# A 4 MB zero fill sent from inside the loop over the heads instead of behind it

## Chip, cores, metric

One core of one Trainium2 chip. The metric is device time in microseconds (us) of one execution. Times are medians, and a comparison is always with runs of the kernel before on the same chip in the same rounds.

## The reference

One decode step of a transformer block and its gradients. Attention has 16 query heads on 8 key/value heads, a cache of 32768 positions of which only the last 4096 are read, and a gated MLP follows. Of the nine outputs two are large: the gradients of the K and V caches, 8 x 32768 x 256 bf16 each. Outside the last 4096 positions they are zero, and these zeros must be written.

```python
W = min(4096, max(256, Sk // 4))                    # 4096 of Sk = 32768
k = jnp.repeat(k_cache[:, :, Sk - W:, :], rep, axis=1)
v = jnp.repeat(v_cache[:, :, Sk - W:, :], rep, axis=1)
scores = jnp.einsum("bhqd,bhkd->bhqk", q, k) * (Dh ** -0.5)
p = _softmax(scores, axis=-1)
o = jnp.einsum("bhqk,bhkd->bhqd", p, v)
...
_out, _vjp = jax.vjp(_f, A_x, A_k_cache, A_v_cache, A_wq, A_wo, B_w_gate, B_w_up, B_w_down)
_grads = _vjp(grad_out)                             # out_2, out_3: the caches' gradients
```

## The kernel before

Most zero fills are sent by GpSimd from a zero buffer of 128 x 8192. The last 18.9 MB of zeros (five transfers, "late fills") are kept back for SyncE, which also sends nearly all loads and all other stores. Four of them read a zero buffer of twice the width; its second half holds data of a V cache until a late memset ("the clearing") makes it zero.

```python
zeros = ar(0, ZW)                                   # ZW = 8192 columns; the second half is ar(ZW, ZW)
late_jobs = [(out_2, G - 1, 5, 7, 2 * ZW), (out_3, G - 1, 0, 6, 2 * ZW), (out_3, G - 1, 6, 7, ZW)]
...                                                 # cut: first pass, MLP, gradients of the small tensors
plan = [[], [], [job_o(0)], [job_o(1)], [job_d, job_q], [expand_dg, job_qB, job_g(0)], [job_g(1)], []]
order = [2, 3, 4, 5, 6, 7, 0, 1]
for it, g in enumerate(order):                      # second pass, one key/value head each
    ...                                             # cut: stV, stK computed by TensorE, VectorE, ScalarE
    for o_ap, st_ in ((out_3, stV), (out_2, stK)):
        LD.dma_start(out=o_ap[0, g, Sk - W:, :].rearrange("(p t) d -> p t d", t=T), in_=st_)
    for job in plan[it]:
        job()                                       # gradients of the weights, made and stored in between
    if it == 6:
        nc.vector.memset(ar(ZW, ZW), 0.0)           # the clearing
...                                                 # cut: GpSimd's last fills
for o, g, n0, n1, f in late_jobs:
    reg = zero_rows(o, g, n0, n1, f)
    for i in range(reg.shape[0]):
        LD.dma_start(out=reg[i], in_=ar(2 * ZW - f, f))
```

`LD` is SyncE's queue; its ring is the line in which its transfers wait for the DMA engines. The two stores of a head are called its pair, and pairs are counted in the order of the loop. The builder is the part of the framework that orders each engine's instructions when the program is built. The drain is the end of the kernel, when nothing computes and the last transfers run.

Of the kernel before, what the change touches and what calls it, by code (L numbers as in the profile page):

```python
# [26 lines left out]
ZW = 8192  # L27
# [7 lines left out]
def kernel(  # L35
# [3 lines left out]
    LD = nc.sync  # L39
# [15 lines left out]
    def ar(off, n):  # L55
        return arena[:, off:off + n]

    def kv_at(off):
        return ar(off, T * Dh).rearrange("p (t d) -> p t d", d=Dh)
# [57 lines left out]
    def zero_rows(o, g, n0, n1, f):  # L117
        reg = o[0, g, 0:Sk - W, :].rearrange("s d -> (s d)")[n0 * 128 * ZW:n1 * 128 * ZW]
        return reg.rearrange("(n p f) -> n p f", p=128, f=f)

    late_jobs = [(out_2, G - 1, 5, 7, 2 * ZW), (out_3, G - 1, 0, 6, 2 * ZW), (out_3, G - 1, 6, 7, ZW)]
    fills = []
    for g in range(G):
        for o in (out_2, out_3):
# [125 lines left out]
    def fill_vpad(i, src):  # L250

        nc.vector.tensor_copy(out=vpad[i][:].rearrange("p e (c w) -> p e c w", w=18)[:, :, :, 0:2],
                              in_=src.unsqueeze(2).to_broadcast([128, 2, 8, 2]))

    def dots(X_sb, XT_slots, pad, rows, cols_pool, cols_tag, evac):

        rows_ps = ps_s.tile([16, 512], f32, tag="rows")
        for q in range(8):
            XT = XT_slots[q % 3]
            tr_ps = ps_tr.tile([128, 2, 4, 128], bf16, tag="tr")  # L260
            for dh in range(2):
                for i in range(4):
                    nc.tensor.transpose(tr_ps[:, dh, i, :], X_sb[:, 4 * q + i, dh * 128:(dh + 1) * 128], ident_bf[:])  # L263
            evac(q, XT, tr_ps[:])
            for dh in range(2):
                nc.tensor.matmul(rows_ps[:], lhsT=pad[:, dh, 16 * q:16 * q + 16], rhs=XT[:, dh].rearrange("p t k -> p (t k)"),  # L266
                                 start=(q == 0 and dh == 0), stop=(q == 7 and dh == 1))
        nc.vector.tensor_copy(out=rows, in_=rows_ps[:])  # L268
        cols_ps = cols_pool.tile([128, 4, 8, 2], f32, tag=cols_tag, name="cols_ps")
        for i in range(4):  # L270
            nc.tensor.transpose(cols_ps[:, i].rearrange("p c h -> p (c h)"), rows[:, i * 128:(i + 1) * 128], ident_f[0:16, 0:16])
        return cols_ps
# [232 lines left out]
    with tc.tile_pool(name="work2", bufs=2) as work2, tc.tile_pool(name="lnw", bufs=1) as lnw, \  # L505
# [109 lines left out]
        for it, g in enumerate(order):  # L615
            V_sb = kv_at(V2_off[it])
            fill_vpad(it % 2, doT_bf[:, :, 2 * g:2 * g + 2])

            def evac(q, XT, ps):
                if q % 2:  # L620
                    nc.scalar.copy(out=XT, in_=ps)  # L621
                else:
                    nc.vector.tensor_copy(out=XT, in_=ps)  # L623
            dpT_ps = dots(V_sb, VT_slot, vpad[it % 2], rows2, ps_t, "tmp", evac)

            pds = work2.tile([128, 4, 8, 4], bf16, tag="pds")
            pv = pT_all[:, g].rearrange("p (q l) h -> p q l h", q=4)
            tmp = work2.tile([128, T, 2], f32, tag="tmp2")
            nc.vector.tensor_tensor(out=tmp[:], in0=dpT_ps[:].rearrange("p q l h -> p (q l) h"),
                                    in1=delta_bc[:, 2 * g:2 * g + 2].unsqueeze(1).to_broadcast([128, T, 2]), op=ALU.subtract)  # L630
            nc.vector.tensor_copy(out=pds[:, :, :, 0:2], in_=pv)
            nc.vector.tensor_tensor(out=pds[:, :, :, 2:4], in0=tmp[:].rearrange("p (q l) h -> p q l h", q=4), in1=pv, op=ALU.mult)
            r_ps = ps_t.tile([128, 128], bf16, tag="tmp")
            nc.tensor.transpose(r_ps[:], pds[:].rearrange("p q l i -> p (q l i)"), ident_bf[:])
            rTm = rT_slot[it % 2]
            nc.vector.tensor_tensor(out=rTm, in0=r_ps[:].unsqueeze(1).to_broadcast([128, 8, 128]),
                                    in1=tl_f[:].unsqueeze(2).to_broadcast([128, 8, 128]), op=ALU.mult)
            nc.vector.tensor_copy(out=Zr, in_=Z4[:, :, :, g, :].rearrange("p w e i -> p (w e) i").unsqueeze(2).to_broadcast([128, 4, 32, 4]))
            R_ps = ps_t.tile([128, 2, 2, 128], f32, tag="tmp")
            for w in range(2):  # L640
                for dh in range(2):
                    nc.tensor.matmul(R_ps[:, w, dh, :], lhsT=Zr[:, 2 * w + dh].rearrange("p k i -> p (k i)"), rhs=ident_bf[:], start=True, stop=True)
            R_sb = R_slot[it % 2]
            nc.scalar.copy(out=R_sb, in_=R_ps[:].rearrange("p w e n -> p (w e n)"))
            stV, stK = V_sb, kv_at(dK_off[it % 2])
            for l in range(8):
                for qp in range(2):
                    d_ps = ps_d.tile([128, 2, 2, Dh], f32, tag="d")
                    for qi in range(2):
                        q = 2 * qp + qi  # L650
                        nc.tensor.matmul(d_ps[:, qi].rearrange("p w d -> p (w d)"), lhsT=rTm[32 * q:32 * (q + 1), l, :], rhs=R_sb[32 * q:32 * (q + 1), :],  # L651
                                         start=True, stop=True)
                    t = 4 * l + 2 * qp
                    if qp:
                        nc.scalar.copy(out=stV[:, t:t + 2, :], in_=d_ps[:, :, 0, :])  # L655
                        nc.scalar.copy(out=stK[:, t:t + 2, :], in_=d_ps[:, :, 1, :])  # L656
                    else:
                        nc.vector.tensor_copy(out=stV[:, t:t + 2, :], in_=d_ps[:, :, 0, :])  # L658
                        nc.vector.tensor_copy(out=stK[:, t:t + 2, :], in_=d_ps[:, :, 1, :])  # L659
# [3 lines that stand above are left out]
                job()  # L663
            if it == 6:

                nc.vector.memset(ar(ZW, ZW), 0.0)

        o, g, i = fills[-1]
        flat = zero_rows(o, g, i, i + 1, ZW)[0].rearrange("p f -> (p f)")
        base = 0  # L670
        for p0, k, m, w in ((0, 5, 2, 288), (20, 3, 8, ZW), (64, 8, 9, ZW - 40), (0, 4, 8, ZW)):
            n = k * m * w
            ZQ.dma_start(out=flat[base:base + n].rearrange("(k m f) -> k m f", k=k, m=m),
                         in_=zeros[p0:p0 + 4 * k - 3:4, 0:w].unsqueeze(1).to_broadcast([k, m, w]))
            base += n
        assert base == 128 * ZW
        for o, g, n0, n1, f in late_jobs:
            reg = zero_rows(o, g, n0, n1, f)
            for i in range(reg.shape[0]):
                LD.dma_start(out=reg[i], in_=ar(2 * ZW - f, f))  # L680

# [1 line left out]
_INS = ['A_x', 'A_k_cache', 'A_v_cache', 'A_wq', 'A_wo', 'B_x', 'B_w_gate', 'B_w_up', 'B_w_down', 'grad_out']  # L683
# [26 lines left out]
```

## Time and profile before

| | before |
|---|---|
| median of 3 runs | 793.49 us (793.12 to 794.23) |
| bytes moved by DMA | 334.75 MB at 423 GB/s |
| DMA engines busy, by stretches of 20 us or more | 0.98 to 1.03 from 20 to 780 us |
| TensorE / VectorE busy | 60% / 52% of the span |
| first late fill sent | 674.95 us |
| the other four sent | 743.93 us |

Read it from the bytes: nothing computes after about 743.5 us, the DMA engines nearly always have work, and the time is nearly bytes over rate. The lines are in the prediction.

### The profile page before, as it was taken

How to read it: one execution, taken by the hardware profiler on the slowest of the kernel's cores; microseconds unless marked ns; L12 is line 12 of the kernel's file. 1: busy time of each engine (PE TensorE's matmuls, PEld its weight loads, DVE VectorE, ACT ScalarE, POOL GpSimd, SP SyncE). 2: the span in 40 equal slices, each digit the busy share in tenths (PEclk: the TensorE clock that was granted, in tenths of full speed). 3: DMA queues.
4: the chain of work that ended last, by engine and by line, in shares of the span. 5: the costliest groups of instructions: out<-in, count | busy, mean ns of one | idle time of the engine just before them, and what ended most of it. 6: DMA issues, size and time to landing. Idle time of an engine off the chain costs nothing.

```text
span 791.1 us, 7239 instructions
## 1 busy us (share of the span) xinstructions
PE 475.9 (60%) x2926; PEld 220.8 (28%) x2926; DVE 410.6 (52%) x621; ACT 196.1 (25%) x309; POOL 29.8 (4%) x41
## 2 busy tenths in 40 slices
PE   0359998999999999453226848583551535363100
PEld 0224333344343433142114714231210211131000
DVE  2105764847658476052884288486680583555300
ACT  0043123141241301000101207372331344134300
POOL 6000000000000000110300000000000000001000
PEclk9987999999999999655556959886556556556555
DMA  9999999999999999999999999999999999999998
GB/s 345 429 432 430 429 430 431 432 431 432 428 427 430 427 427 426 418 420 422 433 431 425 425 425 432 427 429 430 427 426 429 428 427 429 423 428 407 413 439 350
DMA packets 28759, 334.75 MB, mean 423 GB/s; under 512 B 1966, under 2 KB 5046, under 8 KB 6966
## 3 DMA queue, kind: packets, MB, share of 16 engines
q0 software_dynamic: 15904, 216.01, 64.2%
q1 hardware_dynamic: 11382, 116.68, 35.1%
q10 hardware_dynamic: 1440, 1.61, 0.6%
q8 instruction: 23, 0.38, 0.2%
q14 instruction: 10, 0.08, 0.0%
HBM read 53.69 MB, written 280.59 MB: 423 GB/s over the span
## 4 chain that ended last, share of the span: by engine, by line
another core or an unknown queue 40%; DMA 25%; DVE 14%; PE 10%; issue 2%; POOL 2%; ACT 1%; DVEq 0%; ACTq 0%; SPq 0%; POOLq 0%
DMA out_dram<-arena 25%; DVE arena L469 2%; PE rows_ps L266 2%; DVE arena L658 2%; DVE arena L554 2%; PE dqb_ps L512 2%; DVE arena L659 2%; PE d_ps L651 2%; PE tr_ps L263 1%; DVE arena L524 1%; DVE arena L438 1%; POOL out_dram L138 1%; PE dqb_ps L515 1%; DVE arena L623 1%
## 5 line engine op out<-in xcount | busy, mean ns | idle before, releaser
L322 DVE TENSOR_TENSOR arena<-arena,p_f 128x2048 bf16<-128x2048 bf16 x64 | 145.4, 2287 | 64.3 <-PE M_ps L327 64.2
L327 PE MATMUL M_ps<-arena 128*128 128x512 bf16 x512 | 129.3, 381 | 0.2 <-ACT arena L333 0.2
L651 PE MATMUL d_ps<-arena 32*128 32x512 bf16 x256 | 45.4, 521 | 100.6 <-DVE arena L659 85.7
L263 PE MATMUL tr_ps<-ident_bf,arena 128*128 128x128 bf16 x1024 | 92.2, 241 | 20.2 <-DMA arena<-in_A_k_cache_dram 12.7
L266 PE MATMUL rows_ps<-arena,vpad 128*16 128x512 bf16 x256 | 89.5, 445 | 21.4 <-DVE arena L623 15.9
L263 PEld LDWEIGHTS <-arena 128*128 128x128 bf16 x1024 | 68.3, 107 | 74.2 <-issue 60.3
L280 ACT COPY arena<-tr_ps 128x1024 bf16<-128x1024 bf16 x64 | 61.8, 1015 | 70.5 <-PE tr_ps L263 70.5
L330 PE MATMUL ok_ps<-arena 128*16 128x512 bf16 x256 | 64.0, 381 | 0.9 <-DVE arena L307 0.9
L655 ACT CAST arena<-d_ps 128x512 bf16<-128x512 f32 x64 | 37.7, 589 | 106.1 <-PE d_ps L651 106.1
L327 PEld LDWEIGHTS <-arena 128*128 128x128 bf16 x512 | 43.3, 99 | 59.2 <-issue 23.4
L621 ACT COPY arena<-tr_ps 128x1024 bf16<-128x1024 bf16 x32 | 32.5, 1016 | 109.9 <-PE tr_ps L263 35.8
L658 DVE CAST arena<-d_ps 128x512 bf16<-128x512 f32 x64 | 43.9, 686 | 18.2 <-PE d_ps L651 17.7
L659 DVE CAST arena<-d_ps 128x512 bf16<-128x512 f32 x64 | 43.6, 681 | 15.5 <-DMA out_dram<-arena 15.5
L651 PEld LDWEIGHTS <-arena 32*128 32x128 bf16 x256 | 10.7, 96 | 126.0 <-issue 81.9
L656 ACT CAST arena<-d_ps 128x512 bf16<-128x512 f32 x64 | 38.1, 595 | 16.8 <-DMA out_dram<-arena 16.8
L266 PEld LDWEIGHTS <-vpad 128*16 128x16 bf16 x256 | 18.7, 91 | 58.4 <-issue 50.6
L330 PEld LDWEIGHTS <-arena 128*16 128x16 bf16 x256 | 19.1, 89 | 41.6 <-issue 20.5
L549 DVE TENSOR_SCALAR arena<-arena,xT 128x1792 bf16<-128x1792 bf16 (+1 forms) x9 | 7.7, 881 | 37.1 <-DMA out_dram<-arena 37.1
L295 ACT ACTIVATE e_f<-cols_ps,nbias 128x32 f32<-128x32 f32 x16 | 4.5, 286 | 86.9 <-DVE nbias L291 86.9
L524 DVE CUSTOM_DVE_ANT_0 arena<-arena 128x4096 bf16<-128x4096 bf16 x3 | 13.1, 4421 | 23.7 <-ACT arena L517 23.7
L268 DVE COPY arena<-rows_ps 16x512 f32<-16x512 f32 x16 | 10.8, 676 | 27.7 <-PE rows_ps L266 27.7
L623 DVE COPY arena<-tr_ps 128x1024 bf16<-128x1024 bf16 x32 | 21.8, 683 | 3.0 <-PE tr_ps L263 2.5
(198 smaller groups left out, 382.2 us busy)
## 6 DMA issues: line engine op xcount, KB each, us to landing
out_dram<-arena POOLq DMA_DIRECT2D x11, 14336.0 KB, 196.1
out_dram<-arena SPq DMA_DIRECT2D x18, 2048.0 KB, 25.6
out_dram<-arena POOLq DMA_DIRECT2D x15, 2048.0 KB, 54.2
arena<-in_A_v_cache_dram SPq DMA_DIRECT2D x10, 2048.0 KB, 52.8
arena<-in_A_k_cache_dram SPq DMA_DIRECT2D x8, 2048.0 KB, 31.3
out_dram<-arena SPq DMA_DIRECT2D x4, 4096.0 KB, 26.1
out_dram<-arena POOLq DMA_DIRECT2D x1, 12288.0 KB, 43.0
out_dram<-arena POOLq DMA_DIRECT2D x1, 8192.0 KB, 337.3
```

Source lines behind the costliest of these rows:

```text
L263: nc.tensor.transpose(tr_ps[:, dh, i, :], X_sb[:, 4 * q + i, dh * 128:(dh + 1) * 128], ident_bf[:])
L266: nc.tensor.matmul(rows_ps[:], lhsT=pad[:, dh, 16 * q:16 * q + 16], rhs=XT[:, dh].rearrange("p t k -> p (t k)"), start=(q == 0 and dh == 0 ...
L280: sT_ps = dots(kv_at(K_off[g]), KT_slot, vpad[g % 2], rows1, ps_c, "cols", lambda q, XT, ps: nc.scalar.copy(out=XT, in_=ps))
L322: nc.vector.tensor_tensor(out=pK, in0=K_sb[:, 4 * c:4 * c + 4, :].unsqueeze(2).to_broadcast([128, 4, 2, Dh]), in1=p_f[:, c::8, :].unsqueez ...
L327: nc.tensor.matmul(M_ps[:, vh, :], lhsT=V_sb[:, t, vh * 128:(vh + 1) * 128], rhs=pK[:, i, :, :].rearrange("p h d -> p (h d)"), start=(t == ...
L330: nc.tensor.matmul(ok_ps[:].rearrange("p k d -> p (k d)"), lhsT=ppad[g % 2][:, 8 * (t % 4) + t // 4, :], rhs=both(g, t), start=(g == 0 and ...
L621: nc.scalar.copy(out=XT, in_=ps)
L651: nc.tensor.matmul(d_ps[:, qi].rearrange("p w d -> p (w d)"), lhsT=rTm[32 * q:32 * (q + 1), l, :], rhs=R_sb[32 * q:32 * (q + 1), :], start ...
L655: nc.scalar.copy(out=stV[:, t:t + 2, :], in_=d_ps[:, :, 0, :])
L656: nc.scalar.copy(out=stK[:, t:t + 2, :], in_=d_ps[:, :, 1, :])
L658: nc.vector.tensor_copy(out=stV[:, t:t + 2, :], in_=d_ps[:, :, 0, :])
L659: nc.vector.tensor_copy(out=stK[:, t:t + 2, :], in_=d_ps[:, :, 1, :])
```

## The change

The intent is to move one of five late fills out of the tail, into the seventh of eight heads, so that the DMA engines have bytes while the last heads are computed.

```diff
+    late = []
+    for o, g, n0, n1, f in late_jobs:
+        reg = zero_rows(o, g, n0, n1, f)
+        late += [reg[i] for i in range(reg.shape[0])]
...
                 nc.vector.memset(ar(ZW, ZW), 0.0)
+                LD.dma_start(out=late[0], in_=ar(0, 2 * ZW))
...
-        for o, g, n0, n1, f in late_jobs:
-            reg = zero_rows(o, g, n0, n1, f)
-            for i in range(reg.shape[0]):
-                LD.dma_start(out=reg[i], in_=ar(2 * ZW - f, f))
+        for reg in late[1:]:
+            LD.dma_start(out=reg, in_=ar(2 * ZW - reg.shape[1], reg.shape[1]))
```

## The prediction

> **What bounds the kernel now.** I read four views, from coarse to fine. First the page: slices in time, DMA queues and bytes.
>
> ```profile
> DMA  9999999999999999999999999999999999999998
> DMA packets 28759, 334.75 MB, mean 423 GB/s; under 512 B 1966, under 2 KB 5046, under 8 KB 6966
> q0 software_dynamic: 15904, 216.01, 64.2%
> q1 hardware_dynamic: 11382, 116.68, 35.1%
> HBM read 53.69 MB, written 280.59 MB: 423 GB/s over the span
> ```
>
> The row of nines says that the 16 DMA engines are busy in each of the 40 slices, while the page gives TensorE 60% and VectorE 52% of the span. The two queues together take 99.3% of what the DMA engines have; q0 is the one GpSimd fills (the zero fills of the caches' unused part), q1 the one SyncE fills. So the kernel is a stream of 334.75 MB, and time is bytes over rate. To see whether there are holes near the place of the change I cut the last 150 us into stretches.
>
> ```profile
> core 0: us, PE busy (x) PEld busy (x) DVE busy (x) ACT busy (x) POOL busy (x), PEclk, DMA share, GB/s
> 20.00:200.00 180.00, 154.22 (x995) 67.94 (x995) 90.74 (x103) 51.09 (x74) 2.05 (x3) 0.96 1.01 430
> ...
> 660.00:680.00 20.00, 6.44 (x41) 2.72 (x39) 8.93 (x13) 6.59 (x8) 0.00 (x0) 0.67 1.00 426
> 680.00:700.00 20.00, 8.43 (x44) 3.65 (x43) 7.60 (x15) 2.06 (x3) 0.00 (x0) 0.59 1.03 435
> 700.00:720.00 20.00, 15.22 (x103) 7.03 (x102) 14.52 (x25) 11.43 (x19) 2.40 (x4) 0.67 0.98 414
> 720.00:740.00 20.00, 4.56 (x30) 0.90 (x28) 8.87 (x14) 7.62 (x14) 0.00 (x0) 0.50 1.02 415
> 740.00:760.00 20.00, 0.76 (x8) 0.11 (x4) 2.58 (x4) 2.15 (x4) 0.00 (x0) 0.50 1.00 425
> 760.00:780.00 20.00, 0.00 (x0) 0.00 (x0) 0.00 (x0) 0.00 (x0) 0.00 (x0) 0.50 0.99 426
> 780.00:791.10 11.10, 0.00 (x0) 0.00 (x0) 0.00 (x0) 0.00 (x0) 0.00 (x0) 0.50 0.68 289
> ```
>
> The last two columns are what to read: the DMA share stays at 0.98 to 1.03 until 780 us, and only the last 11.1 us have slack (0.68). From about 743 us no engine computes; the kernel drains its last stores and fills.
>
> **Where the fill stands before the change.** The source puts all late fills behind the loop over the heads. The trace shows something else. SyncE's issues in time (start, duration, line):
>
> ```profile
> 652.28 0.33 SPq L609 DMA_DIRECT2D out_dram<-arena  x1
> 674.95 0.33 SPq L680 DMA_DIRECT2D out_dram<-arena  x1
> 675.54 2.32 SPq L661 DMA_DIRECT2D out_dram<-arena  x2
> ...
> 720.87 1.64 SPq L661 DMA_DIRECT2D out_dram<-arena  x2
> ...
> 742.93 0.95 SPq L661 DMA_DIRECT2D out_dram<-arena  x2
> 743.93 5.08 SPq L680 DMA_DIRECT2D out_dram<-arena  x4
> ```
>
> Line 680 is the late fill, line 661 the pair of K and V stores of one head. There are five late fills: four go out at 743.93, behind the last pair, but the first goes out at 674.95, ahead of the pair at 675.54; three pairs of the eight follow it, so that is the sixth head's. The source's order is not the order in which SyncE sends; the framework orders instructions when the program is built, and a fill whose data are ready is free to go. The waits say what held it:
>
> ```profile
> SPq L680 <- DVE arena L666: 22.3, 1, 22.3
> ```
>
> Line 666 is the clearing of the second half of the zero buffer (VectorE, 671.46 to 674.93 in the timeline). SyncE stood 22.3 us before the fill, from the issue at 652.28, and sent it as soon as the clearing ended. So the fill is already sent at the earliest moment at which its data exist.
>
> **What the Trainium skill says.** "DMA: Bandwidth & Descriptors", section "Rules for kernel authors": spreading DMAs over the issuing engines does not add bandwidth, since all run on the same 16 DMA engines. This trace agrees: the first stretch above, with most bytes from GpSimd's queue, moves 430 GB/s, and the last full one, with SyncE's queue alone, 426. The same page, "Queues, rings and completion order": each DMA engine takes turns between the queues with work, and consumes one queue's descriptors in ring order. So a fill sent earlier would stand in front of SyncE's later stores. "HBM Reference", "Access": a core that streams alone gets about 425 GB/s, bounded by its DMA engines; the measured mean is 423. "Perfetto Trace Analysis", "Summary: the profiler window per engine type": the record of a DMA issued by SyncE does not contain the movement of data. Here the issue at 674.95 has 0.33 us, while the landings of such fills took 21.9 to 42.2 us; the order of issues is therefore what to compare, not their durations. No page that I read bears on the builder's order.
>
> **The change, part by part.** Intended: out of the tail goes one fill of 128 x 16384 bf16 = 4.19 MB; at the 426 GB/s of the stretch 760:780 that is 9.8 us of DMA time. It comes in during the seventh head, behind the clearing. Nothing is added: same transfers, same bytes, the same buffer.
> What happens: I built both kernels and compared their programs engine by engine. Each has 6847 instructions, with equal operations, operands, addresses, semaphore waits and order; only line numbers and the running numbers in the names of instructions and PSUM tiles differ (one statement earlier shifts the numbering by one). In both, SyncE's list reads:
>
> ```
> out_4's third block, out_4's last rows, LATE FILL 4 MB, K and V store, out_6 ..., K and V store, ..., K and V store, three fills of 4 MB, one of 2 MB
> ```
>
> This fits the trace above, where the first late fill follows line 609 (out_4's last rows) and precedes a pair of line 661. So the source change asks for a place that the builder had already chosen. The sum:
> - instructions removed or added: 0, on five engines, 0 us
> - bytes moved: 0 MB more or less, 0 us
> - waits changed: none; the fill waits for the clearing and for a semaphore of earlier transfers in both
> - predicted: 793.49 us (the median of before) + 0 = 793.5 us.
>
> **The rivals.**
> 1. *The change is real and fills a hole.* If the built orders did differ, moving 4.19 MB out of the tail would be worth at most 9.8 us: 783.7 us, minus 1.2%. For it: the drain after the last store is all DMA. Bytes of SyncE's last two stores and four fills are 2 x 2.10 + 3 x 4.19 + 2.10 = 18.9 MB, an estimated 44.3 us at 426 GB/s, and 742.93 + 44.3 = 787.2 is near the end. Against: the fill isn't in this list; the trace has four there, not five. And a hole is needed for it to go into. A bound for anything that leaves the bytes alone: 334.75 MB at the 430 GB/s of the stretch 20:200 is an estimated 778.5 us, so all ramps and tails together are 12.6 us, 1.6% of the span. Even this rival stays within 2%.
> 2. *The fill gets in the stores' way.* Ahead of a pair of stores in the same ring it delays them by 9.8 us, or about twice that while GpSimd's queue takes its turns; buffers come free later and the last two heads slip. For it: VectorE waits on landing stores in this part (11.1 us before the clearing at 671.46). Against: this cost, if it is one, is already in the 793.49 us. And the four last fills are on their way from 749.01 (743.93 + 5.08) and the drain ends near 790, so a store that slips by less than some 40 us needs not set the end while other bytes keep the DMA engines busy. If it came on top, I would expect 793 to 803 us.
> 3. *Same program, another time.* Placement of tensors in HBM or a slower chip could move the time though the program is the same. The three runs of before span 793.12 to 794.23 us, 0.14%; the profiled one took 793.07. A chip with another DMA rate is the only thing I can name that would give more; at 1% less rate, 8 us. Nothing in the profile speaks for it.
>
> **Range and chances.** The centre is the median of before. Repeats lie within 0.6 us of one another; I allow three times that for another chip or session, to each side a little over 2 us: 791.5 to 795.8. A move of over 2% means 15.9 us, more than the bound of 12.6 us that I worked out for gains without fewer bytes; slower by 15.9 us would need a slow session that hits only one of two equal programs. So 1% each, and 98% for within 2%.
>
> **What would show it right or wrong.** Right: the issues of SyncE in the changed trace show one fill of 4 MB shortly behind the clearing (near 675 us), ahead of the sixth head's pair, and four late fills behind the last pair near 744; the same packets (28759 to a few), 334.75 MB, DMA share about 1.0 until 780, and the same wait of the fill on the clearing, about 22 us, under new line numbers (671 on 670). Wrong: five late fills behind the last pair, or a fill at another place among SyncE's issues, or another number of packets, or a span that differs by over 3 us in runs of the same chip. Then the comparison of the built programs would have missed something that the chip sees.

## The result

| | before | after |
|---|---|---|
| median of 6 runs each | 793.19 us (792.81 to 794.23) | 793.64 us (793.24 to 793.89) |
| ratio, 95% interval | | 1.0004 (0.9991 to 1.0017) |

A ratio is the mean time of one kernel's fast runs over that of the other's of the same rounds, so it is not quite the ratio of the medians quoted. The interval holds 1: the same.

SyncE's issues in time, kernel after (start, duration, line; line 671 is the first late fill, 665 a pair, 683 the other late fills):

```profile
654.03 0.33 SPq L613 DMA_DIRECT2D out_dram<-arena  x1
676.69 0.33 SPq L671 DMA_DIRECT2D out_dram<-arena  x1
677.27 2.32 SPq L665 DMA_DIRECT2D out_dram<-arena  x2
...
719.81 4.60 SPq L665 DMA_DIRECT2D out_dram<-arena  x2
...
743.73 0.93 SPq L665 DMA_DIRECT2D out_dram<-arena  x2
744.71 5.09 SPq L683 DMA_DIRECT2D out_dram<-arena  x4
```

The order is that of before: one fill ahead of the sixth head's pair, four behind the last. Each entry shown is 0.8 to 1.75 us later or, at the seventh pair, 1.1 us earlier. Programs with an equal order up to there differ by as much: out_4's last rows (line 613 here) go out at 650.45 us in e1, 650.47 in e2 and 651.04 in e3, and at 652.28 in before. What the fill waited for in the kernel after:

```profile
SPq L671 <- DVE arena L670: 22.3, 1, 22.3
```

And the transfers on its page:

```profile
DMA packets 28760, 334.75 MB, mean 423 GB/s; under 512 B 1967, under 2 KB 5047, under 8 KB 6967
```

The same wait, to the tenth, under the new line numbers, the same bytes, and one packet more (it is in an instruction queue). The DMA share of the kernel after was 0.96 to 1.02 in stretches of 20 us from 640 to 780 us.

### The profile page after: what moved, and what is told of

Its sections match the earlier page's. It is cut to its first block, busy times and chain, and to the rows that moved or that the text cites. A ratio compares the mean times of both kernels' runs of the same rounds, so it can differ in the third digit from the quotient of the medians.

```text
span 791.8 us, 7239 instructions
## 1 busy us (share of the span) xinstructions
PE 470.7 (59%) x2926; PEld 219.4 (28%) x2926; DVE 410.4 (52%) x621; ACT 195.9 (25%) x309; POOL 29.7 (4%) x41
## 2 busy tenths in 40 slices
DMA packets 28760, 334.75 MB, mean 423 GB/s; under 512 B 1967, under 2 KB 5047, under 8 KB 6967
## 4 chain that ended last, share of the span: by engine, by line
another core or an unknown queue 40%; DMA 25%; DVE 14%; PE 9%; issue 2%; POOL 2%; ACT 1%; DVEq 0%; ACTq 0%; SPq 0%; POOLq 0%
DMA out_dram<-arena 25%; DVE arena L473 2%; DVE arena L662 2%; PE dqb_ps L516 2%; DVE arena L558 2%; PE rows_ps L270 2%; DVE arena L663 2%; PE d_ps L655 2%; PE tr_ps L267 1%; DVE arena L528 1%; DVE arena L442 1%; POOL out_dram L142 1%; PE dqb_ps L519 1%; DVE arena L627 1%
## 5 line engine op out<-in xcount | busy, mean ns | idle before, releaser
L267 PE MATMUL tr_ps<-ident_bf,arena 128*128 128x128 bf16 x1024 | 90.0, 237 | 21.2 <-DMA arena<-in_A_k_cache_dram 13.4
L270 PE MATMUL rows_ps<-arena,vpad 128*16 128x512 bf16 x256 | 87.4, 436 | 21.9 <-DVE arena L627 16.1
L528 DVE CUSTOM_DVE_ANT_0 arena<-arena 128x4096 bf16<-128x4096 bf16 x3 | 13.1, 4423 | 24.1 <-ACT arena L521 24.1
```

Of the source, the lines that this page charges most:

```text
L267: nc.tensor.transpose(tr_ps[:, dh, i, :], X_sb[:, 4 * q + i, dh * 128:(dh + 1) * 128], ident_bf[:])
L270: nc.tensor.matmul(rows_ps[:], lhsT=pad[:, dh, 16 * q:16 * q + 16], rhs=XT[:, dh].rearrange("p t k -> p (t k)"), start=(q == 0 and dh == 0 ...
```

## The experiments

The result alone says only that two equal programs take equal time. What stayed open is whether the place of the fill, which before already had, is worth anything. Theory A: it keeps the DMA engines busy and its loss would cost 2 to 10 us. Theory B: the order of transfers in a saturated stream doesn't matter. All results were correct.

### e1: the fill really behind all stores

The source's order isn't binding, a dependence is. A product by zero of two columns ties the zero half to the last head's result (edit to the kernel before):

```diff
+        nc.vector.tensor_scalar(out=ar(2 * ZW - 2, 2), in0=stK[:, T - 1, Dh - 2:Dh], scalar1=0.0, scalar2=None, op0=ALU.mult)
         for o, g, n0, n1, f in late_jobs:
```

> The kernel before with a product by zero of two columns (128x2, about 0.1 us) that makes the zero half depend on the last head's K gradient, so that all five late fills really stand behind all stores; in the build the first fill moves from place 56 to place 66 of SyncE's list. Theory A (the place of the fill is worth something and before already had it: the fill keeps the DMA engines busy while the last heads are computed): 4.19 MB leave the stretch 675 to 743 us, the DMA share of a stretch there falls below 0.95, the last late fill is sent near 740 to 749, and the time rises by 2 to 10 us (at most 4.19 MB / 426 GB/s = 9.8 us). Rival B (a stream of bytes has no preferred order, the stores land earlier without the fill ahead of them and the heads finish earlier by as much): 793.2 us, within 1 us, with the last pair of stores issued several us before 743 us.

Measured: 793.58 us against 793.17, ratio 1.0006 (0.9993 to 1.0018): the same. Besides the fill, one store of out_7 (224 KB) changed its place, to ahead of the seventh pair (697.93 against 722.56); VectorE's and ScalarE's orders are those of before, but for the added product. The issues of e1 (line 661 a pair, 681 the late fills):

```profile
716.53 17.06 SPq L661 DMA_DIRECT2D out_dram<-arena  x4
733.68 6.40 SPq L681 DMA_DIRECT2D out_dram<-arena  x5
```

The first line merges the last two pairs. All pairs were out by 733.6 (716.53 + 17.06), 10.3 us before the kernel before's 743.88 (742.93 + 0.95). Of these, 1.8 us were there before the fill (650.45 against 652.28), so the fill's part is some 8.5 us. The slowest landing of a pair's store was 52.1 us after its issue in before, that of the sixth pair, and 38.3 us in e1. With it a wait of VectorE for that buffer went, first before, then e1 (in brackets the idle time ahead of it and what ended it):

```profile
728.82 0.69 DVE L659 CAST arena<-d_ps 128x512 bf16<-128x512 f32 x1 [6.29 <-DMA out_dram<-arena]
```

```profile
717.97 0.68 DVE L659 CAST arena<-d_ps 128x512 bf16<-128x512 f32 x1
```

So without the fill ahead of them in the ring the stores land earlier, the buffers come free earlier, and the heads end earlier. What it won, the drain gives back. SyncE's final waits for its transfers, first e1, then before:

```profile
SPq L706 <- DMA out_dram<-arena: 50.2, 4, 26.1
```

```profile
SPq L705 <- DMA out_dram<-arena: 40.7, 4, 16.6
```

9.5 us more at the end. The DMA share of e1 was 0.98 to 1.03 in every stretch from 700 to 750 us, so no hole opened. B holds here and A falls: in this program the place is worth nothing that these runs can tell (the interval allows a gain of 0.6 to a loss of 1.4 us).

### e2 and e3: two, and all five, inside the loop

```diff
-                LD.dma_start(out=late[0], in_=ar(0, 2 * ZW))
+                for reg in late[:2]:                # e3: late[:5]
+                    LD.dma_start(out=reg, in_=ar(2 * ZW - reg.shape[1], reg.shape[1]))
...
-        for reg in late[1:]:
+        for reg in late[2:]:                        # e3: late[5:]
```

> The changed kernel with two fills in the loop at the same place of the source; the build leaves the first at place 56 and sends the second between the seventh and the eighth pair of stores. A: holes are already closed by the one fill (DMA share 0.98 to 1.03 before), so nothing is gained: 793 us within 1 us; a small gain of up to 2 us if the 407 to 415 GB/s of 720 to 760 us in before and after come from a lack of large transfers. B: 793.2 us within 1 us.

> All five late fills in the loop; the build sends four of them (14.7 MB, 34.5 us at 426 GB/s) between the seventh and the eighth pair, so that the last pair of stores is the last thing in SyncE's ring. A and B both: bytes are the same and the last pair is still issued near 743 us, when the ring holds more than what is left of the fills, so 793 us within 2 us. A third theory C (fills ahead of stores hold up the heads): the seventh head's buffers come free later only if a later head waits for them; none does after the eighth, so C expects the same as A here. Any time over 797 us would show that the order in the ring matters by itself.

Measured: e2 793.54 us (ratio 1.0006, 0.9994 to 1.0019), e3 793.27 us (1.0006, 0.9992 to 1.0020), against 793.17. Here the source did move transfers: in e3 four fills go out at 723.83, in front of the last pair. Nothing gained, nothing lost. These two runs cannot tell A from B, as both expected it; they show that bytes can change places at the end without cost.

### e4: the clearing on GpSimd

```diff
-                nc.vector.memset(ar(ZW, ZW), 0.0)
+                nc.gpsimd.memset(ar(ZW, ZW), 0.0)
```

> The changed kernel with the clearing of the second zero half on GpSimd in place of VectorE: VectorE no longer stands 11.1 us for the landing store nor spends 3.5 us on it. The build then sends all five late fills behind the last pair, so this joins two things: the fill last, as in e1, and a VectorE without the stop. A: the heads finish up to 14.5 us earlier than in e1, the hole of e1 shrinks, and the time is between before's and e1's: 793 to 798 us. B: 793.2 us within 1 us. If VectorE's stop were what set the end, the time would fall below 790 us.

Measured: 801.03 us against 793.17, ratio 1.0098 (1.0084 to 1.0112; four runs of e4, and likewise of e8 below, five of the others). B is wrong for this one, A's range of 793 to 798 us was missed too, and so was the thought that VectorE's stop at the clearing sets the end: without it the kernel was 7.9 us slower. The DMA share falls to 0.82, 0.56 and 0.69 in the stretches 710 to 720, 720 to 730 and 740 to 750. The deepest (the last columns are the DMA share and GB/s):

```profile
720.00:730.00 10.00, 5.89 (x33) 2.06 (x33) 8.26 (x14) 5.94 (x11) 2.39 (x4) 0.50 0.56 223
```

As in e1 all five fills stand last, but here it costs. Why here and not there was the new question. One edit had changed two things, the engine and the builder's order, so the next runs separate them.

### e6: no clearing, late fills free

The fills read the first zero half twice, so nothing late holds them; the source sends all five behind the loop. (A version e5 with the first fill inside the loop gave the same order on SyncE in the build and was not run.)

```diff
+    def put_late(reg):
+        k = reg.shape[1] // ZW
+        LD.dma_start(out=reg.rearrange("p (k f) -> p k f", k=k), in_=zeros.unsqueeze(1).to_broadcast([128, k, ZW]))
...
-            if it == 6:
-                nc.vector.memset(ar(ZW, ZW), 0.0)
-                LD.dma_start(out=late[0], in_=ar(0, 2 * ZW))
...
-        for reg in late[1:]:
-            LD.dma_start(out=reg, in_=ar(2 * ZW - reg.shape[1], reg.shape[1]))
+        for reg in late:
+            put_late(reg)
```

> The changed kernel without the clearing: the late fills read the first zero half twice, so they depend on nothing that happens late, and the source sends all five behind the loop, as before's source did. The build moves all five (18.9 MB) up to places 32 to 41 of SyncE's list, ahead of and between the loads for the second pass. Theory A (the clearing is what holds the fill at its place; bytes held back are what keeps the DMA engines busy at the end): fills in front of loads delay the second pass by 18.9 MB at 215 to 430 GB/s, 44 to 88 us, and at the end nothing but two stores is left, so the DMA share falls well below 0.9 after about 740 us and the time is 800 to 840 us. B (order is free in a stream of bytes): 793 us within 2 us.

Measured: 796.10 us against 793.20, ratio 1.0042 (1.0028 to 1.0055). Both expectations missed, A's by far. The build did send the fills at 383.85 to 452 us, though the source has them at the very end, and the second pass did slip: its last two pairs went out from 759.03 to 776.67, 33 us later than in before. But no hole opened. Stretches of e6 (last columns: DMA share, GB/s):

```profile
740.00:750.00 10.00, 0.61 (x2) 0.20 (x2) 3.46 (x6) 0.52 (x2) 0.00 (x0) 0.50 1.01 422
750.00:760.00 10.00, 6.66 (x33) 2.31 (x32) 8.68 (x15) 5.42 (x11) 2.40 (x4) 0.50 0.99 406
760.00:780.00 20.00, 4.59 (x32) 0.77 (x28) 10.31 (x16) 8.59 (x16) 0.00 (x0) 0.50 1.02 419
```

With SyncE's fills gone early, GpSimd's fills had to wait: its last large one, sent at 396.65, took 369.8 us to land, so until 766 us, where in before it was sent at 391.33 and took 337.3, until 729 us (that the one is the cause of the other is argued, not tested). These bytes and the slipped stores kept the DMA engines busy at the end. With a second pass that is 33 us late, e6 takes only 2.9 us more. The trace places them at the very end: the DMA share is 1.01 in 778 to 782 us, then 0.38 in 788 to 790 and 0.06 in 790 to 794, and the last store lands at 792.6 us (775.64 + 17.0), where before's last fill landed at 790.0 (747.75 + 42.2). Why the end is longer was not tested; the other form of the fills alone is not it, as e7 has it too and was the same as before.

### e7 and e8: no clearing, with the order fixed

Both are e6 with a constraint on the order of issue (it orders issues on SyncE and waits for nothing). In e7 the first fill follows the fifth pair and the others the last pair; in e8 all five follow the last pair.

```diff
-    def put_late(reg):
+    def put_late(reg, behind):
         k = reg.shape[1] // ZW
-        LD.dma_start(out=reg.rearrange(...), in_=...)
+        with tc.issue_after(behind.ins):
+            LD.dma_start(out=reg.rearrange(...), in_=...)
...
+            if it == 4:                             # e7 alone
+                put_late(late[0], last_store)
...
-        for reg in late:
-            put_late(reg)
+        for reg in late[1:]:                        # e8: late
+            put_late(reg, last_store)
```

> As e6 (no clearing, VectorE neither stands 11.1 us nor spends 3.5 us), but with issue order fixed: the first late fill behind the fifth head's pair of stores (place 54), the other four behind the last pair. A: a fill is in the ring while heads seven and eight are computed, no hole: 793 us within 2 us, with the last pair issued as early as VectorE allows. If e4's 801 us came from the order of stores that a VectorE without the stop brings, and not from the missing fill, this run is near 801 too.

> As e7, but with all five late fills fixed behind the last pair of stores. SyncE's and VectorE's orders are those of e4 without the clearing. A: as e4, a hole of some 8 us while heads seven and eight are computed: 799 to 803 us. B: 793 us within 2 us. If GpSimd's 6.9 us clearing held up its own last fills and that made e4 slow, this run has no such thing and is near 793.

Measured: e7 793.66 us (ratio 1.0004, 0.9992 to 1.0017), e8 799.87 us (1.0085, 1.0071 to 1.0098), against 793.20. So in programs without the stop at the clearing, the two orders differ by 6.2 us (799.87 - 793.66). That this is all the fill's place is not shown by this pair: the builder also moved other stores (out_4's third block goes out at 645.71 us in e8, at 665.54 in e7) and changed VectorE's order. e9 separates them. GpSimd's memset is not the cause, as e8 has none. Stretches of e8 (columns as in the prediction; the last two are the DMA share and GB/s):

```profile
700.00:710.00 10.00, 0.99 (x13) 0.61 (x11) 0.00 (x0) 1.83 (x3) 0.00 (x0) 0.72 0.99 416
710.00:720.00 10.00, 3.44 (x10) 0.81 (x9) 6.30 (x10) 2.15 (x4) 0.00 (x0) 0.50 0.78 313
720.00:730.00 10.00, 4.74 (x30) 1.78 (x29) 8.25 (x14) 5.93 (x11) 2.40 (x4) 0.50 0.64 257
730.00:740.00 10.00, 3.07 (x20) 0.55 (x20) 6.48 (x11) 5.37 (x10) 0.00 (x0) 0.50 0.91 387
740.00:750.00 10.00, 0.61 (x4) 0.11 (x4) 1.42 (x3) 1.07 (x2) 0.00 (x0) 0.50 0.79 331
```

The missing share is 2.2 + 3.6 + 0.9 + 2.1 = 8.8 us, the loss against before 6.7 us. Not every missing share becomes time: e7 has 0.73 in 740 to 750, so 2.7 us are missing, and it was the same as before. The hole is one in supply: in the stretch 700 to 710 VectorE did nothing at all, SyncE sent nothing from 671.6 to 713.8 us, and no late fill was in its ring.

### e9: e4 with the fill put back ahead of the last two pairs

```diff
-                LD.dma_start(out=o_ap[0, g, Sk - W:, :].rearrange(...), in_=st_)
-            for job in plan[it]:
-                job()
-            if it == 6:
-                nc.gpsimd.memset(ar(ZW, ZW), 0.0)
-                LD.dma_start(out=late[0], in_=ar(0, 2 * ZW))
+                with tc.issue_after(first.ins) if it > 5 else nullcontext():
+                    store = LD.dma_start(out=o_ap[0, g, Sk - W:, :].rearrange(...), in_=st_)
+            with tc.issue_after(first.ins) if it == 6 else nullcontext():
+                for job in plan[it]:
+                    job()
+            if it == 5:
+                nc.gpsimd.memset(ar(ZW, ZW), 0.0)
+                with tc.issue_after(store.ins):
+                    first = LD.dma_start(out=late[0], in_=ar(0, 2 * ZW))
```

> As e4 (clearing on GpSimd), with the order of issue fixed so that the first late fill follows out_6's stores and precedes the seventh pair; orders of the four compute engines are those of e4, and on SyncE the fill moves from place 66 to 60 and out_7's first store goes behind the seventh pair. A: the fill is sent near 678 us when GpSimd's clearing ends, its 4.19 MB (9.8 us) fill e4's hole at 710 to 750 us (DMA share 0.82, 0.56, 0.99, 0.69 there): 793 to 796 us. B or a cause on the compute engines: 801 us, as e4.

Measured: 793.43 us against 793.20, ratio 1.0004 (0.9991 to 1.0016), as A expected. VectorE and ScalarE have the same order in e4, e8 and e9; on SyncE, out_7's two stores also changed places, to behind the seventh pair (726.14 and 727.81 us; 715.54 and 718.16 in e4), which takes bytes out of the hole's start and brings none. Stretches of e9, to be held against those of e8:

```profile
710.00:720.00 10.00, 4.35 (x17) 1.17 (x16) 7.27 (x12) 2.54 (x5) 0.00 (x1) 0.50 1.05 435
720.00:730.00 10.00, 4.44 (x29) 1.53 (x28) 7.71 (x14) 5.76 (x12) 2.39 (x4) 0.50 0.98 400
730.00:740.00 10.00, 3.07 (x20) 0.55 (x20) 6.47 (x11) 5.40 (x11) 0.00 (x0) 0.50 0.98 411
740.00:750.00 10.00, 0.00 (x0) 0.00 (x0) 1.00 (x2) 0.83 (x2) 0.00 (x0) 0.50 1.03 428
```

TensorE, VectorE and ScalarE do much the same in these stretches as in e8, and the heads end only a little earlier (last fills sent from 742.13, against 742.58 in e8). VectorE stands for the same store as in e8 (13.1 us). So the hole is closed by the fill, sent at 675.74, and its place is worth 7.6 us here (801.03 - 793.43). Here A is right.

### e10: e8 with one store ahead of the sixth pair

What makes the heads stand in e8 and not in e1? In e1 and before, SyncE sends the store of out_4's last rows ahead of the sixth pair; without the clearing the builder sends it behind (662.71 instead of 650.45 in e1). This edit to e8 makes the rows' job come first:

```diff
-        plan = [..., [expand_dg, job_qB, job_g(0)], [job_g(1)], []]
+        plan = [..., [job_g(0)], [job_g(1)], []]
...
+            if it == 5:
+                expand_dg()
+                rows = job_qB()                     # job_qB now returns its last store
             for o_ap, st_ in ((out_3, stV), (out_2, stK)):
-                last_store = LD.dma_start(...)
+                with tc.issue_after(rows.ins) if it == 5 else nullcontext():
+                    last_store = LD.dma_start(...)
```

> As e8 (no clearing, all five late fills behind the last pair), but the store of out_4's last rows is fixed ahead of the sixth pair of stores, as before, after and e1 have it; SyncE's order is then e1's. VectorE's order differs from e8's in 26 lines of the comparison because the two jobs are traced one step earlier. Theory D (e4 and e8 are slow because out_4's last rows land late behind 4.19 MB of the sixth pair, the out_7 job on VectorE waits for that landing, 19.4 and 13.8 us in e8, and heads seven and eight stand behind it, with no fill in the ring meanwhile): those two waits shrink to some 6 us each, the last pair is issued before 738 us, the DMA share stays over 0.95 from 710 to 750 us, and the time is 793 to 795 us. If the time is 799 us or more, D is wrong and what makes e1 (793.6) differ from e8 (799.9) lies in the clearing on VectorE itself.

Measured: 793.70 us against 793.37, ratio 1.0005 (0.9991 to 1.0018). The out_7 job on VectorE (scaling into a buffer that the two stores of out_4's third block and last rows must have left; in brackets the idle time ahead of it and what ended it), first e8, then e10:

```profile
687.56 1.28 DVE L558 TENSOR_SCALAR arena<-arena,xT 128x1792 bf16<-128x1792 bf16 x2 [19.38 <-DMA out_dram<-arena]
713.10 0.69 DVE L558 TENSOR_SCALAR arena<-arena,xT 128x1792 bf16<-128x1792 bf16 x1 [13.82 <-DMA out_dram<-arena]
```

```profile
688.38 1.28 DVE L558 TENSOR_SCALAR arena<-arena,xT 128x1792 bf16<-128x1792 bf16 x2 [19.59 <-DMA out_dram<-arena]
694.97 0.69 DVE L558 TENSOR_SCALAR arena<-arena,xT 128x1792 bf16<-128x1792 bf16 x1 [4.72 <-DMA out_dram<-arena]
```

The second wait ended at 713.10 in e8 and at 694.97 in e10, 18 us earlier. The trace names the store: of the last rows' store in e8 (line 618, sent at 662.71), `prof e8_no_clear_last --source L618` says who waited for it and how long it took to land:

```profile
  DVE arena L558: 13.8, 1
DMA to landing us min/median/max: 50.4/50.4/50.4
```

662.71 + 50.4 is 713.1, the end of the wait; in e10 it is 652.08 + 42.9 = 695.0. The last pair was out by 734.57 (its merged issues ran from 714.72 for 19.85 us), and the DMA share was 0.91 to 1.03 from 710 to 750 (I had expected over 0.95). The first wait stayed (19.59; I had expected some 6): it is for the store of out_4's third block, which lands at much the same time in all three (687.5 us in e8, 688.3 in e10, 688.1 in before); it is longer than before's 5.68 us because VectorE comes to it earlier. VectorE's order differs somewhat between e8 and e10, so the run does not isolate the one store as cleanly as e9 isolates the fill.

## Why the prediction was right

It gave 793.5 us, range 791.5 to 795.8, and 98% for within 2%; measured 793.64 us. Step by step:

- **Bound by the stream of bytes: right**, for before and after. Both moved 334.75 MB, and six of the nine experiments stayed within 0.5 us of before. Even e6, with a second pass 33 us late, lost only 2.9 us. But e4 and e8 moved as many bytes and lost 7.9 and 6.7 us, with a DMA share down to 0.56 and 0.64: the same bytes do not suffice where the stream has a hole.
- **The fill already stands there: right.** After sends it at 676.69 behind the clearing and ahead of the sixth pair, four others from 744.71; the wait is 22.3 us in both.
- **The sum of 0: right**, to 0.45 us in the medians of six runs each, inside the noise. With equal programs nothing else was to be expected; the test of the stream's slack is in the experiments.
- **The range: right, with a wrong reason.** The repeats that it names lie 1.1 us apart (793.12 to 794.23), not within 0.6, and three times 0.6 is 1.8, not a little over 2.
- **Rival 1, a real move worth up to 9.8 us.** e1 undoes the fill's place for real and costs nothing that the runs show (0.06%, interval 0.9993 to 1.0018). As a claim on this program the rival is wrong. As a mechanism it exists: e4 against e9 gives 7.6 us. What the prediction did not see is the condition, as these runs have it: the place of the fill counts where the stores behind it do not come earlier without it (e4, e8), and not where they do (e1).
- **Rival 2, the fill delays the stores by 9.8 us.** This is what e1 shows: some 8.5 us at the last pair. The wait that goes is the 6.29 us at 728.82, not the 11.1 us before the clearing that the prediction named for it: that one ends before the fill is sent, and e1 still has 11.04. But the final waits change by 9.5 us the other way, and the sum is unchanged. The prediction counted it as a possible cost already in the time; the runs show none.
- **Rival 3, another chip.** The kernel before took 793.17 to 793.37 us on the three chips of the experiments.

No version beat both kernels beyond the noise. The bound of 778.5 us that the prediction estimated was not approached, and what remains at the start and in the last 11 us was not tried.

## What to carry to other kernels

Before asking what a moved line is worth, compare the built orders and the issues in the trace: the builder may have moved it already, and a dependence (here the clearing) fixes the place, not the line in the source. Where the DMA engines were always busy, here, moving a transfer delayed others by about its own length and the drain returned it (e1); look for a stretch where the share falls well below 1 before expecting anything, and even then measure (0.78, 0.64, 0.91 and 0.79 in e8 went with 6.7 us, a single 0.73 in e7 with nothing that shows). When freeing an engine makes a kernel slower, as in e4, look for a changed order of stores and a hole in supply.

## What the Trainium skill lacked or had wrong

- No page says how the order in which a built program issues its DMAs follows from the source's. Here a fill written behind all stores went out at 674.95 us, ahead of stores up to 742.93 us, and without its dependence all five went out from 383.85 us (e6).
- "DMA: Bandwidth & Descriptors", "Rules for kernel authors", advises to issue a DMA early and to wait late. It lacks the limit: with the DMA engines saturated, four more fills ahead of the last pair brought nothing (e3, ratio 1.0006), and all five ahead of and between loads cost 0.42% (e6), where the same form of fills, sent later, was the same as before (e7, ratio 1.0004).
- The same page, "Queues, rings and completion order", has the ring order but no cost for what stands behind: a 4.19 MB fill ahead of later stores moved the end of the heads by some 8.5 us (e1), and an out_4 store sent behind a pair landed after 50.4 us instead of 42.9, with a wait of 13.82 us on VectorE instead of 4.72 (e8 against e10).
